# Reordering the opening of a fused attention-and-mixer kernel: the shift's row, the statistics and the first sums

## The chip, the cores and the metric

The kernel runs on one core of a Trainium2 chip. The core has a matrix engine (TensorE; its matmuls are "PE" in the profile and its weight loads "PEld"), a vector engine (VectorE, "DVE"), an engine for activations (ScalarE, "ACT"), GpSimd ("POOL") and SyncE ("SP"), which here issues most of the transfers. Each engine works through its own list of instructions in order, and engines wait for each other through semaphores. The metric is the device time of one execution in microseconds (us): before the change 448.7 us, the median of three runs from 448.26 to 449.26.

## The reference

The input x has 2048 tokens of 448 channels. Six vectors come from a condition c: `sa, ca, ga, sb, cb, gb`. Cut to what matters here:

```
mod = (silu(c) @ w_mod).reshape(1, 6, 1, 448)
h = layernorm(x) * (1 + ca) + sa
q, k, v = split(h @ wqkv)                     # 16 heads of 28
pq, pk = phi(q), phi(k)                       # phi(t) = t + 1 if t > 0 else exp(t), + 1e-6
o = (pq @ (pk^T v)) / (pq @ sum(pk) + 1e-6)
x = x + ga * (o @ wo)
h = layernorm(x) * (1 + cb) + sb
x = x + gb * mixer(h)                         # a token MLP, gelu between two products
```

The change lies in the first of these lines: the projection of k (the letter j = 1 in the code) and the sum over tokens of pk times the normalised x.

## The kernel before

The tokens are cut into 16 tiles of 128 (`NT`). A tile comes twice from memory: `X[t]` with tokens on the partitions and `XT[t]`, its transpose, in four pieces of channels, the last of 64 channels stored twice. Products are made to nearly full fp32 precision from fp32r halves: a "high" half, the rounded value, and a "low" half, the rest. `a_split(t)` makes `hh` (high, on ACT, L390) and `hl` (low, on DVE, L393) of `XT[t]`.

The layernorm is not applied to the input of the projection. The weights Wk are scaled by 1 + ca (`w_high`, `w_low`, L253 and L265), x itself is multiplied by them (`project(t, 1, "kp")`, ten matmuls, L410), and one more matmul of a few rows, `close(t, 1)` (L417), adds what mean and spread require. On its moving side stand the rows of `Wrow`: the column sums of the scaled weights and the product of the shift sa with Wk, "the shift's row". On its stationary side stand mean and deviation of each token, transposed. After that the tile only needs the factor 1/deviation per token, which `a_exp(t)` gives as a scale: an exp (L424) and a relu (L425) on ACT, read from the PSUM bank of the projection.

The shift's row is made in these steps: `col_acc(0)` (DVE) and `col_mm` (PE, L215 and L217) give sa as columns, `col_out(0)` copies them to SBUF (DVE, L225 to L227), the four `row_part(1, ch)` add Wk times these columns up (DVE, L271 once and L273 three times), `row_sum(1)` (PE, L280) and `row_bias(1)` (PE, L283) sum over the partitions into the bank `rowb`, and `row_out(1)` copies the rows to `Wrow` (ACT, L287) and cuts the second half (DVE, L288).

The statistics of a tile come in two forms. `a_stats_act` uses ACT: a pass that sums (L349), a pass that squares (L328), each with a readout of the accumulator; POOL scales the sums (L354, L355). `a_stats` uses DVE: `bn_stats` and `bn_aggr` (L364, L365) and an addition (L366). Both end in a power on POOL (L340) that gives deviation and its inverse, "the root", for one tile or two at once. Before the change ACT serves tiles 0, 1 and 4 (`ACT_STATS`), DVE all others. `a_rows(t)` writes mean and deviation with their rests into `rowst` (L373, L375): on POOL for the tiles in `ACT_STATS`, on DVE for the others. `a_transpose(t, n)` (PE, L383) turns the rows of one or two tiles in one bank, `a_copy(t)` (ACT, L386) puts them beside `hl` of the tile, where `close(t, 1)` finds them.

After `a_exp(t)`, `a_pk(t)` (DVE, L430) makes pk, `a_pk_parts(t)` its halves `pkh` (ACT, L478) and `pkl` (for tiles 0 and 1 on DVE, L480; for most others ACT and an accumulating transfer issued by POOL, L483), and a second transfer of POOL (L487) adds pk to a running sum. `a_norm(t)` (DVE, L458) normalises `X[t]` to `xn`, `a_high` (ACT, L462) and `a_low` (DVE, L467, L468) make its halves `xh` and `xl`. `a_outer(t)` (PE, L504) is "the sums" of a tile: eleven matmuls into four banks `cacc`, which stay in use until tile 15.

PSUM has eight banks, and each new bank waits until the last reader of its former tile is done; the SBUF tiles come from a pool of 74 slots in the same way. The order on each engine is the order of the program text. What is between the opening matmuls and the loop is written out by hand; then the loop over t from 4 to 15 projects tile t + 1, closes tile t, transposes t + 1, adds the sums of tile t - `KV_LAG` = t - 4, and lets ACT, DVE and POOL prepare the tiles ahead. The order on PE around the change, before it: project(0) to project(2), columns of sa, row_sum, project(3), transposes of 0 and 1, row_bias, transposes of 2 and 3, project(4), close 0 to 3, transpose of 4, and in the loop project(5), close(4), transpose of 5, sums of 0, project(6), close(5), transpose of 6, sums of 1, project(7).

Of the kernel before, what the change touches and what calls it, by code (L numbers as in the profile page):

```python
# [8 lines left out]
F32 = mybir.dt.float32  # L9
# [5 lines left out]
P = 128  # L15
# [12 lines left out]
Q_EARLY = {10: 0, 11: 1, 12: 2, 13: 3, 14: 4}  # L28
ACT_STATS = (0, 1, 4)
RING = 6  # L30
# [18 lines left out]
def block_kernel(ctx: ExitStack, tc: tile.TileContext, x, xt, wqkv, wo, w1, b1, w2, b2, c, wmod, wfirst, out):  # L49
# [29 lines left out]
    def split(full, hi, lo):  # L79
# [15 lines left out]
    nc.gpsimd.affine_select(out=m3, in_=m3, compare_op=ALU.is_ge, fill=0.0, base=DH - 1,  # L95
                            pattern=[[0, 4], [DH, 4], [0, DH]], channel_multiplier=-1)
    mhalf = cst.tile([P, 2], F32, name="mhalf")
    nc.vector.memset(mhalf, -0.5)
# [239 lines left out]
    def a_pow(g, ve):  # L338
        n = g.shape[1]
        nc.gpsimd.tensor_tensor(g[:, :, 1:3], ve, roots.unsqueeze(1).to_broadcast([P, n, 2]), op=ALU.pow)  # L340
# [18 lines left out]

    def a_stats(*ts):  # L360
        g, ve = a_group(ts)
        for t in ts:
            b6 = small.tile([P, 6], F32, name=f"st{t}", tag="st")
            nc.vector.bn_stats(b6, X[t])  # L364
            nc.vector.bn_aggr(mv[t][:, 0:2], b6)  # L365
        nc.vector.tensor_scalar_add(ve, g[:, :, 1:2].to_broadcast([P, len(ts), 2]), EPS)  # L366
        a_pow(g, ve)

    def a_rows(t):
        r = rowst[t % RING]  # L370
        pair = mv[t][:, 0:2]
        eng = nc.gpsimd if t in ACT_STATS else nc.vector
        eng.tensor_copy(r[:, 64:].rearrange("p (b c) -> p b c", b=2)[:, :, 0:2],  # L373
                              pair.unsqueeze(1).to_broadcast([P, 2, 2]))
        eng.tensor_sub(r[:, 66:68], pair, r[:, 64:66].bitcast(F32))  # L375

# [19 lines left out]
    def a_split(t):  # L396
        a_split_high(t)
        a_split_low(t)
# [13 lines left out]
    def project(t, j, name):  # L412
        projects([(t, kind, ch) for ch in range(3) for kind in ("hh", "wl", "hl")] + [(t, "hh", 3)], j, name)
# [111 lines left out]
    w_row(1)  # L525
    act2, act2_end = a_stats_act((0, 1))
    act2(0)
    col_acc(0)
# [3 lines left out]
    a_split(3)  # L532
    act2(1)
    act2_end()
    a_rows(0)
    a_rows(1)
    a_stats(2, 3)
    col_out(0, pc)
    for ch in range(4):
        row_part(1, ch)  # L540
    project(3, 1, "kp")
    a_transpose(0, 2)
    row_bias(1)
    a_split(4)
    a_rows(2)
    a_rows(3)
    act1, act1_end = a_stats_act((4,))
    act1(0)
    act1_end()
    a_rows(4)  # L550
    a_norm(0)
    a_stats(5)
    a_copy(0)
    a_copy(1)
    a_high(0)
    row_out(1)
    a_transpose(2, 2)
    load_xt(9)
# [3 lines left out]
    load_x(10)  # L562
    project(4, 1, "kp")
    a_copy(2)
    a_copy(3)
    a_split_high(5)
    a_low(0)
    a_split_low(5)
    kps = [close(t, 1) for t in range(4)]
    a_transpose(4)  # L570
    a_exp(0, kps[0])
    a_copy(4)
    a_rows(5)
    a_pk(0, kps[0])
    a_norm(1)
    a_pk_parts(0)
    a_exp(1, kps[1])
    a_pk(1, kps[1])
    a_stats(6)
    a_exp(2, kps[2])  # L580
    a_split_high(6)
    a_exp(3, kps[3])
    a_pk(2, kps[2])
    a_split_low(6)
    a_high(1)
    a_pk_parts(1)
    a_rows(6)
    a_low(1)
    a_pk(3, kps[3])
# [4 lines left out]
    for t in range(4, NT):  # L594
        if t + 1 < NT:
            project(t + 1, 1, "kp")
        kp = close(t, 1)
        if t + 1 < NT:
            a_transpose(t + 1)
        if t == 9:  # L600
            row_sum(0)
            row_bias(0)
        a_outer(t - KV_LAG)
        if t in Q_EARLY:
# [10 lines left out]
        a_phi_q(t in Q_EARLY)  # L615
        if t + 1 < NT:
            a_copy(t + 1)
# [635 lines left out]
```

## Time and profile before

| What | us |
|---|---|
| median of three runs | 448.7 |
| lowest and highest run | 448.26, 449.26 |
| the profiled execution's own time | 449.38 |
| its span in the trace | 447.7 |
| PE busy in it | 440.4 |
| DVE busy in it | 353.7 |
| ACT busy in it | 266.0 |
| POOL busy in it | 106.7 |

A row of a timeline gives the start and the duration in us, then the engine, the line of the kernel, the operation, the tile written and the tiles read, the shape, the count of merged instructions, and in brackets the idle time of the engine ahead of it with what ended that idle time. Durations of pipelined instructions overlap: from start to start is the time that an engine is occupied. The granted TensorE clock of the profiled execution is 1.0.

### The profile page before, as it was taken

The page shows a single profiled execution, that of the slowest core. Times are in us where ns is not written, and L with a number is a line of the kernel's source. Part 1 is how long each engine was busy: PE and PEld are TensorE (multiplying, and loading weights), DVE is VectorE, ACT ScalarE, POOL GpSimd, SP SyncE. Part 2 cuts the span into 40 slices and gives each one's busy share as a digit, 9 for nine tenths or more (in the row PEclk, how much of TensorE's full clock was granted, in tenths as well). Part 3 has the DMA queues.
Part 4 walks back from the last instruction along what each step waited for, and adds up shares of the span by engine and source line. Part 5 has one row for each costly group of instructions (what it writes and reads, how often), then busy time and mean ns, then how long its engine had stood idle before and what let it go on. Part 6 is the DMA issues. An engine that isn't in the chain of part 4 may idle for free.

```text
span 447.7 us, 7324 instructions
## 1 busy us (share of the span) xinstructions
PE 440.4 (98%) x2370; PEld 405.4 (91%) x2370; DVE 353.7 (79%) x798; ACT 266.0 (59%) x575; POOL 106.7 (24%) x195
## 2 busy tenths in 40 slices
PE   8989999999999999999999999999999999999997
PEld 7868889999899999989999999999999999999996
DVE  3978998679998899896467776649697788978873
ACT  4679978657757776767674444336554546356531
POOL 3346454300024355454300000000110211302101
PEclk9999999999999999999999999999999999999999
DMA  7997999545200003322416454227985668966333
GB/s 239 383 290 137 218 241 250 84 141 191 72 1 1 23 25 96 71 48 48 141 32 217 158 164 140 90 76 240 283 190 156 111 187 196 213 175 116 54 89 62
DMA packets 58854, 63.22 MB, mean 141 GB/s; under 512 B 5249, under 2 KB 49345, under 8 KB 58817
## 3 DMA queue, kind: packets, MB, share of 16 engines
q1 hardware_dynamic: 51616, 51.17, 37.6%
q0 software_dynamic: 7200, 11.60, 16.1%
q8 instruction: 18, 0.29, 0.3%
q14 instruction: 20, 0.16, 0.1%
HBM read 46.57 MB, written 7.34 MB: 120 GB/s over the span
## 4 chain that ended last, share of the span: by engine, by line
PE 92%; DMA 2%; ACT 2%; POOL 1%; SPq 1%; issue 1%; DVE 0%; ACTq 0%; POOLq 0%
PE y L1009 14%; PE up L817 10%; PE up L819 10%; PE up L818 10%; PE op L766 9%; PE cacc L504 7%; PE qp L410 7%; PE y L1010 7%; PE kp L410 5%; PE yp L817 3%; PE yp L818 2%; PE yp L819 2%; PE tq L750 2%; DMA wr<-in_qkv_dram 1%; DMA x<-in_A_x_dram 1%; PE qp L417 1%
## 5 line engine op out<-in xcount | busy, mean ns | idle before, releaser
L817 PE MATMUL up<-h2h,ph 128*128 128x448 f32 x224 | 81.3, 363 | 0.0
L819 PE MATMUL up<-h2h,pl 128*128 128x448 f32 x224 | 81.2, 363 | 0.0
L818 PE MATMUL up<-h2l,ph 128*128 128x448 f32 x224 | 80.8, 361 | 0.0
L81 DVE TENSOR_TENSOR pl<-pr,ph 128x512 fp32r<-128x512 f32 (+1 forms) x60 | 36.3, 616 | 14.2 <-ACT ph L80 10.3
L80 ACT ACTIVATE ph<-pr 128x512 fp32r<-128x512 f32 (+1 forms) x60 | 33.0, 570 | 24.0 <-PE up L818 17.7
L819 PEld LDWEIGHTS up<-h2h,pl 128*128 128x128 f32 x224 | 42.0, 188 | 3.1
L818 PEld LDWEIGHTS up<-h2l,ph 128*128 128x128 f32 x224 | 41.9, 187 | 3.0
L817 PEld LDWEIGHTS up<-h2h,ph 128*128 128x128 f32 x224 | 42.0, 188 | 2.4
L971 POOL DMA_DIRECT2D a<-a x12 | 10.6, 912 | 113.1 <-PE yp L819 97.0
L1029 POOL DMA_DIRECT2D out_dram<-yt x12 | 10.5, 872 | 83.1 <-DVE yt L1020 54.7
L1015 ACT ACTIVATE cc<-y 128x448 f32<-128x448 f32 x18 | 9.8, 546 | 25.5 <-PE y L1010 25.5
L766 PE MATMUL op<-wph,pth 112*128 112x448 f32 x64 | 24.5, 382 | 0.0
L504 PE MATMUL cacc<-pkh,xh 128*128 128x448 f32 x64 | 24.4, 381 | 0.0
L410 PE MATMUL kp<-wh,hh 128*128 128x448 f32 x64 | 23.0, 369 | 1.1 <-ACT rk L425 0.9
L410 PE MATMUL qp<-wh,hh 128*128 128x448 f32 x64 | 23.4, 365 | 0.0
L504 PE MATMUL cacc<-pkl,xh 128*128 128x448 f32 x64 | 23.3, 364 | 0.0
L766 PE MATMUL op<-wpl,pth 112*128 112x448 f32 x64 | 23.3, 363 | 0.0
L766 PE MATMUL op<-wph,ptl 112*128 112x448 f32 x64 | 23.2, 362 | 0.0
L754 ACT ACTIVATE pth<-tq 112x512 fp32r<-112x512 f32 x16 | 9.6, 599 | 17.6 <-PE tq L750 17.6
L817 PE MATMUL yp<-uw,qw 128*128 128x448 f32 x54 | 19.9, 369 | 0.0
L819 PE MATMUL yp<-uw,qw 128*128 128x448 f32 x54 | 19.6, 364 | 0.0
L818 PE MATMUL yp<-uw,qw 128*128 128x448 f32 x54 | 19.6, 363 | 0.0
(243 smaller groups left out, 1311.2 us busy)
## 6 DMA issues: line engine op xcount, KB each, us to landing
pr<-in_B_w_dram SPq DMA_DIRECT2D x48, 256.0 KB, 3.0
a<-in_B_w_dram SPq DMA_DIRECT2D x24, 256.0 KB, 5.3
a<-in_B_w_dram SPq DMA_DIRECT2D x24, 192.0 KB, 5.4
xt<-in_xt_dram SPq DMA_DIRECT2D x16, 256.0 KB, 4.9
x<-in_A_x_dram SPq DMA_DIRECT2D x16, 224.0 KB, 4.8
wm<-in_B_wmod_dram SPq DMA_DIRECT2D x16, 196.0 KB, 5.0
wr<-in_qkv_dram SPq DMA_DIRECT2D x12, 224.0 KB, 5.5
out_dram<-x SPq DMA_DIRECT2D x12, 224.0 KB, 2.0
```

The source lines that it names most:

```text
L80: nc.scalar.activation(hi, full, AF.Copy)
L81: nc.vector.tensor_sub(lo, full, hi.bitcast(F32))
L410: nc.tensor.matmul(pps[t, j][:, :D], a[:, ch * P:(ch + 1) * P], w, start=first, stop=False)
L504: nc.tensor.matmul(cacc[ch][:, :D], a[:, s], b, start=(t == 0 and i == 0), stop=(t == NT - 1 and i == len(todo) - 1))
L766: nc.tensor.matmul(opb[t][:, :D], a[:, s], b, start=(n == 0), stop=(n == 11))
L817: nc.tensor.matmul(ps[:, :D], hi[:, sl], mh, start=first, stop=False)
L818: nc.tensor.matmul(ps[:, :D], hi[:, sl], ml, start=False, stop=False)
L819: nc.tensor.matmul(ps[:, :D], lo[:, sl], mh, start=False, stop=last)
L971: nc.gpsimd.dma_start(w, a, accum_op=ALU.add)
L1009: nc.tensor.matmul(ps[:, :D], h[:, s], w, start=opens and r == 0, stop=False, skip_group_check=True)
L1010: nc.tensor.matmul(ps[:, :HD], l[:, s], wh, start=False, stop=closes and r == PAIRS - 1, skip_group_check=True)
L1029: nc.gpsimd.dma_start(of[t * P:(t + 1) * P, :], ysum.pop(t), accum_op=ALU.add)
```

## The change

The tiles' statistics change engines: ACT takes tiles 2 and 3, DVE takes tile 4 in one group with tile 5 (`a_stats_dve`, which splits the work into a part for each tile and an end with one root for both). All rows are now written by DVE. `col_out(0)` and the additions with Wk (`row_part`) keep their place after the statistics of tiles 0 and 1, but the statistics of tiles 2 and 3 on DVE are no longer ahead of them. Project(4), then the closing of tiles 0 and 1, come ahead of the transposes of 2 and 3; project(5) ahead of the closing of 2 and 3; the sums of tile 0 ahead of the transposes of tiles 4 and 5 (now a pair in one bank) and of project(6); close(4) after project(6). What the loop did in its turn t = 4 for PE, and project(6) of turn 5, is written out ahead of it. A tile of 160 bytes named `space` that nothing uses takes the room that the dropped small tiles leave, so that the addresses of the later tiles are those of before. The order on PE after it: project(3), transposes of 0 and 1, row_bias, project(4), close 0 and 1, transposes of 2 and 3, project(5), close 2 and 3, sums of 0, transposes of 4 and 5, project(6), close(4), close(5), transpose of 6, sums of 1, project(7).

```diff
--- before.py
+++ after.py
@@ -26,7 +26,6 @@
 KV_LAG = 4
 HIGH_AT = {13: (11, 12), 14: (13,), 15: (14, 15)}
 Q_EARLY = {10: 0, 11: 1, 12: 2, 13: 3, 14: 4}
-ACT_STATS = (0, 1, 4)
 RING = 6
 FETCH = {4: 11, 5: 12, 7: 13, 9: 14, 10: 15}
 SUM_DMA = range(2, 13)
@@ -94,6 +93,7 @@
                             pattern=[[0, 4], [-DH, 4], [0, DH]], channel_multiplier=1)
     nc.gpsimd.affine_select(out=m3, in_=m3, compare_op=ALU.is_ge, fill=0.0, base=DH - 1,
                             pattern=[[0, 4], [DH, 4], [0, DH]], channel_multiplier=-1)
+    cst.tile([P, 40], F32, name="space")
     mhalf = cst.tile([P, 2], F32, name="mhalf")
     nc.vector.memset(mhalf, -0.5)
     roots = cst.tile([P, 2], F32, name="roots")
@@ -357,22 +357,30 @@
             a_pow(g, ve)
         return one, end
 
-    def a_stats(*ts):
+    def a_stats_dve(ts):
         g, ve = a_group(ts)
-        for t in ts:
-            b6 = small.tile([P, 6], F32, name=f"st{t}", tag="st")
-            nc.vector.bn_stats(b6, X[t])
-            nc.vector.bn_aggr(mv[t][:, 0:2], b6)
-        nc.vector.tensor_scalar_add(ve, g[:, :, 1:2].to_broadcast([P, len(ts), 2]), EPS)
-        a_pow(g, ve)
+
+        def one(i):
+            b6 = small.tile([P, 6], F32, name=f"st{ts[i]}", tag="st")
+            nc.vector.bn_stats(b6, X[ts[i]])
+            nc.vector.bn_aggr(mv[ts[i]][:, 0:2], b6)
+
+        def end():
+            nc.vector.tensor_scalar_add(ve, g[:, :, 1:2].to_broadcast([P, len(ts), 2]), EPS)
+            a_pow(g, ve)
+        return one, end
+
+    def a_stats(t):
+        one, end = a_stats_dve((t,))
+        one(0)
+        end()
 
     def a_rows(t):
         r = rowst[t % RING]
         pair = mv[t][:, 0:2]
-        eng = nc.gpsimd if t in ACT_STATS else nc.vector
-        eng.tensor_copy(r[:, 64:].rearrange("p (b c) -> p b c", b=2)[:, :, 0:2],
+        nc.vector.tensor_copy(r[:, 64:].rearrange("p (b c) -> p b c", b=2)[:, :, 0:2],
                               pair.unsqueeze(1).to_broadcast([P, 2, 2]))
-        eng.tensor_sub(r[:, 66:68], pair, r[:, 64:66].bitcast(F32))
+        nc.vector.tensor_sub(r[:, 66:68], pair, r[:, 64:66].bitcast(F32))
 
     tps = {}
 
@@ -523,84 +531,93 @@
               (1, "wl", 0), (1, "wl", 1), (1, "wl", 2), (1, "hl", 0), (1, "hl", 1), (1, "hl", 2)], 1, "kp")
     project(2, 1, "kp")
     w_row(1)
-    act2, act2_end = a_stats_act((0, 1))
-    act2(0)
+    act01, end01 = a_stats_act((0, 1))
+    act01(0)
     col_acc(0)
     pc = bank("col0")
     col_mm(pc, macc.pop(0), one, True, True)
     row_sum(1)
     a_split(3)
-    act2(1)
-    act2_end()
-    a_rows(0)
-    a_rows(1)
-    a_stats(2, 3)
+    act01(1)
+    end01()
     col_out(0, pc)
     for ch in range(4):
         row_part(1, ch)
+    a_rows(0)
+    a_rows(1)
     project(3, 1, "kp")
     a_transpose(0, 2)
     row_bias(1)
     a_split(4)
+    a_norm(0)
+    dve45, end45 = a_stats_dve((4, 5))
+    dve45(0)
+    act23, end23 = a_stats_act((2, 3))
+    act23(0)
+    act23(1)
+    end23()
+    a_copy(0)
+    a_copy(1)
+    row_out(1)
     a_rows(2)
     a_rows(3)
-    act1, act1_end = a_stats_act((4,))
-    act1(0)
-    act1_end()
-    a_rows(4)
-    a_norm(0)
-    a_stats(5)
-    a_copy(0)
-    a_copy(1)
     a_high(0)
-    row_out(1)
-    a_transpose(2, 2)
     load_xt(9)
     load_x(9)
     load_mod(2)
     load_xt(10)
     load_x(10)
     project(4, 1, "kp")
+    a_split(5)
+    a_low(0)
+    kps = [close(t, 1) for t in (0, 1)]
+    a_transpose(2, 2)
+    project(5, 1, "kp")
+    a_exp(0, kps[0])
+    a_pk(0, kps[0])
+    dve45(1)
+    end45()
     a_copy(2)
     a_copy(3)
-    a_split_high(5)
-    a_low(0)
-    a_split_low(5)
-    kps = [close(t, 1) for t in range(4)]
-    a_transpose(4)
-    a_exp(0, kps[0])
-    a_copy(4)
-    a_rows(5)
-    a_pk(0, kps[0])
+    kps += [close(t, 1) for t in (2, 3)]
+    a_exp(1, kps[1])
     a_norm(1)
     a_pk_parts(0)
-    a_exp(1, kps[1])
+    a_outer(0)
     a_pk(1, kps[1])
-    a_stats(6)
+    a_rows(4)
+    a_rows(5)
+    a_transpose(4, 2)
     a_exp(2, kps[2])
     a_split_high(6)
-    a_exp(3, kps[3])
     a_pk(2, kps[2])
     a_split_low(6)
+    a_exp(3, kps[3])
     a_high(1)
+    a_copy(4)
+    a_copy(5)
+    project(6, 1, "kp")
+    kps.append(close(4, 1))
+    a_stats(6)
     a_pk_parts(1)
+    a_low(1)
     a_rows(6)
-    a_low(1)
     a_pk(3, kps[3])
     a_pk_parts(2)
     a_stats(7)
     wo_sb = []
     late = [t for t in range(NT) if t not in Q_EARLY.values()]
     for t in range(4, NT):
-        if t + 1 < NT:
+        if 5 < t < NT - 1:
             project(t + 1, 1, "kp")
-        kp = close(t, 1)
-        if t + 1 < NT:
+        kp = close(t, 1) if t > 4 else kps[4]
+        if 4 < t < NT - 1:
             a_transpose(t + 1)
         if t == 9:
             row_sum(0)
             row_bias(0)
-        a_outer(t - KV_LAG)
+        if t > 4:
+            a_outer(t - KV_LAG)
         if t in Q_EARLY:
             a_q(Q_EARLY[t])
         if t == 12:
@@ -613,7 +630,7 @@
         if 7 < t + 3 < NT:
             a_stats(t + 3)
         a_phi_q(t in Q_EARLY)
-        if t + 1 < NT:
+        if 4 < t < NT - 1:
             a_copy(t + 1)
         a_exp(t, kp)
         if t + 3 < NT:
```

## The prediction

> **What bounds the kernel now.** I read the page first, then the waits of PE (TensorE's matmuls), then the timelines of the engines between 16 and 45 us. All times are us from the start of the span; "tile t" is token tile t.
>
> ```profile
> span 447.7 us, 7324 instructions
> ...
> PE 440.4 (98%) x2370; PEld 405.4 (91%) x2370; DVE 353.7 (79%) x798; ACT 266.0 (59%) x575; POOL 106.7 (24%) x195
> ```
>
> PE is busy for 98% of the span, so an edit that leaves PE's work as it is can win only where PE stands still. The waits of PE over the whole span say where:
>
> ```profile
> PE kp L410 <- ACT rk L425: 0.9, 1, 0.9
> PE rw L383 <- DVE rowst L373: 0.9, 1, 0.9
> ```
>
> Beside the first matmul of the span and two waits of 0.3 us or less before 11 us, the list has only these two and one for POOL's rows, which the timeline below splits into 0.27 and 0.40. All of it, 2.4 us, lies in the stage that the diff rewrites (the bracket is the idle time before the row and what ended it):
>
> ```profile
> 21.05 0.37 PE L410 MATMUL kp<-wh,hh 128*128 128x448 f32 x1
> 21.68 0.32 PE L383 MATMUL rw<-ident,rowst 128*98 128x128 f32 x1 [0.27 <-POOL rowst L375]
> 22.40 0.32 PE L383 MATMUL rw<-ident,rowst 128*98 128x128 f32 x1 [0.40 <-POOL rowst L375]
> 22.55 0.92 PE L283 MATMUL rowb<-accb,sel_b 128*98 128x448 f32 x2
> 24.32 0.50 PE L383 MATMUL rw<-ident,rowst 128*98 128x128 f32 x2 [0.86 <-DVE rowst L373]
> ...
> 26.77 1.08 PE L417 MATMUL kp<-wrow,hl 98*128 98x448 f32 x4
> ...
> 30.49 0.47 PE L504 MATMUL cacc<-pkl,xh 128*128 128x448 f32 x1
> ...
> 33.63 0.48 PE L410 MATMUL kp<-wh,hh 128*128 128x448 f32 x1 [0.87 <-ACT rk L425]
> ...
> 39.15 0.47 PE L410 MATMUL kp<-wh,hl 128*128 128x448 f32 x1
> ```
>
> Project(3) ends at 21.25 (its last matmul starts at 21.05 and the next could start 0.2 later). The transposes of tiles 0 and 1 wait for POOL's rows, those of tiles 2 and 3 for DVE's; project(6) waits until exp(3) has read its bank. The row at 39.15 is the third matmul of project(7); I measure the lead there. The chain of waits gives the price of PE's work when nothing is missing:
>
> ```profile
> 45.89 2.21 PE cacc L504 x11
> 48.09 2.03 PE kp L410 x10
> ```
>
> So a matmul of 448 columns is 0.20, a projection 2.03, the eleven sums of a tile 2.21. The two pairs follow each other without a gap, and the list of PE's waits has nothing later than 33.63: what PE gains before project(7) should reach the end of the span.
>
> **Part 1: the shift's row earlier.** The diff takes the statistics of tiles 2 and 3 off DVE (they go to ACT), so that col_out(0) and the four additions follow straight after a_split(3). Rows 0 and 1 go from POOL to DVE.
>
> ```profile
> 17.54 0.27 PE L217 MATMUL col<-ones,acc 128*64 128x128 f32 x1
> ```
> ```profile
> 17.58 0.62 DVE L364 BATCH_NORM_STATS2 st<-x 128x6 f32<-128x448 f32 x1
> ...
> 19.48 0.16 DVE L226 COPY col<-col 128x3 f32<-128x3 f32 x1
> ...
> 20.17 2.12 DVE L273 SCALAR_TENSOR_TENSOR accb<-wr,col,accb 128x448 f32<-128x448 f32 x3
> ...
> 23.81 0.17 DVE L373 CAST rowst<-mv 128x4 fp32r<-128x4 f32 x1 [0.92 <-POOL mv L340]
> 24.02 0.16 DVE L375 TENSOR_TENSOR rowst<-mv,rowst 128x2 fp32r<-128x2 f32 x1
> 24.09 0.16 DVE L373 CAST rowst<-mv 128x4 fp32r<-128x4 f32 x1
> ```
> ```profile
> 18.89 1.29 POOL L340 TENSOR_TENSOR mv<-ve,roots 128x4 f32<-128x4 f32 x1
> ```
>
> DVE is free at 17.58; the column that it copies is complete on PE at 17.81. I start the copy at 17.95 in place of 19.48; from there to the end of the additions is 22.29 - 19.48 = 2.81, so they end at 20.76. The roots of tiles 0 and 1 are there at 20.18. A tile's row costs DVE 0.28 (23.81 to 24.09) and PE's transpose starts 0.30 after the second instruction of a row (24.02 to 24.32). Row 0 starts at 20.68, row 1 at 20.96, its second instruction at 21.17: transposes at 21.27 and 21.5 instead of 21.68 and 22.40, the biased row at 21.65 instead of 22.55. PE is free again at the latest 0.92 after that; I take 22.5 for project(4), which needs nothing of tiles 2 and 3 and ends at 24.53.
>
> **Part 2: closing 0 and 1 first.** Close(0) needs the row copied out by ACT, then cut by DVE, behind the statistics that ACT got:
>
> ```profile
> 18.34 0.19 ACT L328 ACTIVATION_READ_ACCUMULATOR junk<-x,as 128x1 f32 x1
> ...
> 18.95 0.56 ACT L349 ACTIVATE junk<-x 128x448 f32<-128x448 f32 x1
> ...
> 20.45 0.19 ACT L328 ACTIVATION_READ_ACCUMULATOR junk<-x,as 128x1 f32 x1
> 22.75 0.44 ACT L386 ACTIVATE hl<-rw 34x128 fp32r<-34x128 f32 x2 [2.11 <-PE rw L383]
> ...
> 25.51 0.54 ACT L287 ACTIVATE wrow<-rowb 34x448 fp32r<-34x448 f32 x1
> ```
> ```profile
> 26.09 0.63 DVE L288 TENSOR_TENSOR wrow<-rowb,wrow 2x448 fp32r<-2x448 f32 x1 [0.25 <-ACT wrow L287]
> ```
>
> One tile's statistics occupy ACT for about 1.6 (18.95 to 20.54). Two end at 22.13, where ACT stands idle now (the bracket of 2.11), so the added tile costs nothing; without that idle time it would cost 1.6. Two copies end at 22.58, the row leaves ACT at about 23.35 and DVE at 24.0: 0.5 before project(4) ends. POOL needs 1.65 from the end of ACT's last read (18.53 to 20.18 for tiles 0 and 1), so the roots of 2 and 3 are there at 23.9, and DVE's rows 2 and 3 at 24.5. PE then runs without a wait: close 0 and 1 from 24.53, two transposes, project(5) from 25.25 to 27.28, close 2 and 3 to 27.68.
>
> **Part 3: the first sums ahead of tile 4.** They need tile 0 to go through the whole chain:
>
> ```profile
> 27.34 0.64 ACT L424 ACTIVATE ek<-kp,mv 128x448 f32<-128x448 f32 x1 [0.30 <-PE kp L417]
> 27.87 0.63 ACT L425 ACTIVATE rk<-kp,mv 128x448 f32<-128x448 f32 x1
> ```
> ```profile
> 28.54 0.63 DVE L430 SCALAR_TENSOR_TENSOR pk<-ek,rk 128x448 f32<-128x448 f32 x1 [0.22 <-ACT rk L425]
> ...
> 29.81 0.63 DVE L480 SCALAR_TENSOR_TENSOR pkl<-pk,pkh 128x448 fp32r<-128x448 f32 x1 [0.22 <-ACT pkh L478]
> ```
>
> Close(0) to exp(0) is 0.57 (26.77 to 27.34), and exp and relu take 0.53 each of ACT's time (27.34 to 27.87). So exp(0) at 25.10, ACT free at 26.16; then the copies of 2 and 3 (0.45), exp(1) (1.06), and pkh(0) from 27.67 to 28.25, and pkl(0) follows it on DVE by 0.03: 28.28 to 28.91. The second sum starts 0.05 after that (30.44 to 30.49): 28.95. Behind close(3) PE therefore idles from 27.68 to 28.95, less 0.2 for the first sum: this order makes a **new wait of about 1.1**, and the transposes of 4 and 5 and project(6) are queued behind it. The remaining ten sums and a hiccup end at 31.05, two transposes at 31.35. A root of 4 and 5 begun at about 27.9 is done at 29.2, the rows at 29.9, so they are in time. Project(6) needs the bank that exp(2) or exp(3) reads; behind pkh(0) ACT has both, with one other copy between, done by 30.8. It starts at 31.35 against 33.63: 2.28 less, of which close(4) is still owed (0.2).
>
> From here DVE, not PE, sets the pace, because its low half of tile 7 arrives just when PE wants it:
>
> ```profile
> 36.51 0.62 DVE L364 BATCH_NORM_STATS2 st<-x 128x6 f32<-128x448 f32 x1
> ...
> 37.45 0.51 DVE L458 TENSOR_SCALAR xn<-x,mv 128x448 f32<-128x448 f32 x1
> 37.88 0.62 DVE L430 SCALAR_TENSOR_TENSOR pk<-ek,rk 128x448 f32<-128x448 f32 x1
> 38.42 0.68 DVE L393 TENSOR_TENSOR hl<-xt,hh 128x512 fp32r<-128x512 f32 x1
> ```
>
> Statistics take 0.94 of DVE, xn 0.43, pk 0.54, hl 0.6. After pkl(0) DVE has pk(1), rows 4 and 5, pk(2), hl6 and statistics 6 (to 32.1), pkl(1) behind ACT's copies of 4 and 5 (32.6 to 33.1), low(1) 0.6, row 6 0.28, pk(3), statistics 7, xn(2), pk(4): hl7 from 36.5 to 37.15, against 38.42 to 39.10. PE has project(6) to 33.38, two closes to 33.8, transpose 6 at 34.1, the sums to 36.45, and its third matmul of project(7) at 36.85 must wait for 37.15. **Lead at that row: 39.15 - 37.15 = 2.0.** DVE's moved work cancels: two tiles' statistics leave it (1.7), one comes (0.8) with three rows (0.84).
>
> The unused 160-byte tile is never written and costs nothing; the loads keep their order on SP's queue. Bounds of what the trace doesn't show: the new wait could shrink to 0.6 (pkh(0) alone) or grow by the 0.6 that a root can lengthen (rows below). Lead 1.4 to 2.5.
>
> On POOL next to DVE the trace has two roots of one tile:
>
> ```profile
> 25.91 0.72 POOL L340 TENSOR_TENSOR mv<-ve,roots 128x2 f32<-128x2 f32 x1 [0.26 <-DVE ve L366]
> ...
> 37.71 1.33 POOL L340 TENSOR_TENSOR mv<-ve,roots 128x2 f32<-128x2 f32 x1
> ```
>
> The second overlaps pk(4) and hl7 above: it is 0.6 longer, while DVE's two keep 0.62 and 0.68. The Trainium skill ("SBUF — State Buffer", Who interferes with whom) says that a VectorE instruction with two SBUF inputs and a GpSimd one that reads SBUF exclude each other, the later one blocked until the first ends. By that rule pkl(0) would wait out the root of 4 and 5, and the lead would be 1.0; the trace agrees for POOL's side only, so my sum leaves DVE free.
>
> **The rivals.**
> - **POOL's root holds DVE.** A root begun at 27.9 keeps pkl(0), two SBUF inputs, until 29.2: the second sum at 29.9 instead of 28.95, 0.95 lost, lead 1.05, time 447.65. For it: the 0.6 above shows that they interfere. Against it: in the rows DVE lost nothing.
> - **The lead is given back.** In the loop's later turns accumulating DMAs hold DVE:
>
> ```profile
> 73.27 0.63 DVE L430 SCALAR_TENSOR_TENSOR pk<-ek,rk 128x448 f32<-128x448 f32 x1 [1.45 <-DMA pk<-pk]
> ```
>
>   If those landings stay where they are while all else comes 2.0 earlier, waits grow by 2.0 and the time is 448.7. Against it: this 1.45 costs PE nothing today, and those DMAs are issued behind work that moves too.
> - **Slower: tile slots run short in turns 5 to 8.** The new order keeps other tiles alive, and a wait like that of 1.45 on DVE would there have no cover, since hl7 comes 0.05 before PE takes it. Two of them cost 2.9 against 2.0 won: 449.6. It decides once such waits before 58 us exceed 2.0. Against it: today the first one on DVE comes after 60 us, and the tiles of a turn are the same.
>
> **How the numbers follow.** The profiled execution took 449.38, its span 447.7 with 1.7 around it; the sum makes it 447.4. That run is 0.7 above the median of 448.7, so the forecast is 448.7 - 2.0 = 446.7. A change of 0.2% (0.9 us) is about what a measurement here can tell from none. Chances: forecast 0.62 (own range 446.2 to 447.3, from the leads), POOL's root 0.15, given back 0.11, slower 0.12. Faster 0.77, same 0.11, slower 0.12. The range, 445.9 to 448.2, takes in the first rival and the better half of the second.
>
> **What would show it.** Right: transposes 0 and 1 before 21.7, project(4) before 22.7 with no idle time until close(3), one wait of about 1.1 at the first sums, released by ACT's pkh and DVE's pkl, project(6) near 31.4, the third matmul of project(7) near 37.2, PE's later timeline the same and 2.0 earlier. Wrong: pkl(0) starting only at the end of POOL's root; DVE waits for DMAs before 58; a wait of close(0) for the row's cut on DVE; a first sum later than 30.

## The result and the profile after

| | median, us | range, us | runs | ratio to the kernel before, 95% interval |
|---|---|---|---|---|
| before | 448.44 | 447.96 to 449.59 | 20 | |
| after | 447.38 | 446.86 to 448.55 | 20 | 0.9976 [0.9969, 0.9983] |

The changed kernel is faster by 1.06 us, 0.24%. The forecast was 446.7 and a lead of 2.0: the direction is right and the time lies in the range, but half of the lead is missing. The profiled execution of the kernel after took 448.35, its span 446.2.

The page and the list of PE's waits (us in total, times, the longest), kernel after:

```profile
span 446.2 us, 7331 instructions
...
PE 439.1 (98%) x2370; PEld 405.5 (91%) x2370; DVE 353.5 (79%) x801; ACT 267.5 (60%) x580; POOL 104.3 (23%) x188
```
```profile
PE kp L418 <- ACT wh L253: 1.1, 1, 1.1
...
PE cacc L512 <- ACT pkh L486: 0.3, 1, 0.3
PE rw L391 <- DVE rowst L383: 0.3, 1, 0.3
...
PE cacc L512 <- DVE pkl L488: 0.2, 1, 0.2
```

The waits of 0.9, 0.9 and 0.7 for exp(3)'s bank, DVE's rows and POOL's rows are gone. In their place stand the new wait at the first sums, in two parts, and a short one for a row. Of the lines left out (`...`) two matter little to the stage: 0.6 ahead of the columns of the opening (0.2 before), and a new 0.2 at a transpose behind 117 us. One number grew with which the diff has nothing to do: the first projection waits 1.1 for the split weights, where the profile of before had 0.3. The timeline of PE, kernel after (start, duration, and in the bracket the idle time before the row and what ended it):

```profile
11.43 0.47 PE L418 MATMUL kp<-wh,hh 128*128 128x448 f32 x1 [1.10 <-ACT wh L253]
...
22.18 0.43 PE L391 MATMUL rw<-ident,rowst 128*98 128x128 f32 x2
22.45 0.92 PE L283 MATMUL rowb<-accb,sel_b 128*98 128x448 f32 x2
22.85 0.71 PE L418 MATMUL kp<-wh,hh 128*128 128x448 f32 x1
23.40 0.37 PE L418 MATMUL kp<-wl,hh 128*128 128x448 f32 x1
...
28.09 0.57 PE L425 MATMUL kp<-wrow,hl 98*128 98x448 f32 x2
29.00 0.47 PE L512 MATMUL cacc<-pkh,xh 128*128 128x448 f32 x1 [0.34 <-ACT pkh L486]
29.66 0.47 PE L512 MATMUL cacc<-pkl,xh 128*128 128x448 f32 x1 [0.19 <-DVE pkl L488]
...
31.91 0.45 PE L418 MATMUL kp<-wh,hh 128*128 128x448 f32 x1
...
34.92 0.29 PE L391 MATMUL rw<-ident,rowst 128*98 128x128 f32 x1 [0.33 <-DVE rowst L383]
...
37.87 0.47 PE L418 MATMUL kp<-wh,hl 128*128 128x448 f32 x1
```

From the transposes of 0 and 1 to the closing of 3 there is no bracket, as forecast (the third matmul of project(5) starts 0.31 behind the second in place of 0.20, so 0.1 is lost there). Behind that closing (28.09, two matmuls, so the next could start at 28.49) the first sum starts at 29.00 and the second, possible at 29.20, at 29.66: 0.51 and 0.46, together 0.97 of idle time against the forecast's 1.07. The third matmul of project(7) is at 37.87 where it was 39.15: 1.28 earlier. What follows it keeps that: from it to the end of the span are 408.55 before (447.7 - 39.15) and 408.33 after (446.2 - 37.87).

Everything in this timeline before 28 us is later than forecast, because this execution opened later. The two kernels' rows of the opening, ACT's and PE's timelines, before:

```profile
7.76 0.63 ACT L390 ACTIVATE hh<-xt 128x512 fp32r<-128x512 f32 x1 [3.61 <-DMA xt<-in_xt_dram]
...
14.72 0.58 ACT L349 ACTIVATE junk<-x 128x448 f32<-128x448 f32 x1 [1.55 <-DMA x<-in_A_x_dram]
```
```profile
10.50 0.47 PE L410 MATMUL kp<-wh,hh 128*128 128x448 f32 x1 [0.28 <-ACT wh L253]
```

and ACT's timeline after:

```profile
8.69 0.63 ACT L398 ACTIVATE hh<-xt 128x512 fp32r<-128x512 f32 x1 [4.55 <-DMA xt<-in_xt_dram]
...
15.17 0.58 ACT L349 ACTIVATE junk<-x 128x448 f32<-128x448 f32 x1 [1.07 <-DMA x<-in_A_x_dram]
```

Two loads set these two openings. The first split waits for XT0's landing (7.76 and 8.69) and the first projection follows it by 2.74 (10.50 and 11.43); the statistics of tile 0 wait for X0's (14.72 and 15.17). Neither load was moved by the diff. The stage from the first projection to the third matmul of project(7) took 28.65 before (39.15 - 10.50) and 26.44 after (37.87 - 11.43). That is 2.21 shorter, a little more than the forecast's 2.0, while the matmul itself came only 1.28 earlier and the medians differ by 1.06. The experiments ask which opening each kernel hangs on, and then which part of the diff carries the gain.

### The profile page after: what moved, and what is told of

It is laid out like the page before. It is cut to its first block, busy times and chain, and to the rows that moved or that the text cites. A ratio compares the mean times of both kernels' runs of the same rounds, so it can differ in the third digit from the quotient of the medians.

```text
span 446.2 us, 7331 instructions
## 1 busy us (share of the span) xinstructions
PE 439.1 (98%) x2370; PEld 405.5 (91%) x2370; DVE 353.5 (79%) x801; ACT 267.5 (60%) x580; POOL 104.3 (23%) x188
## 4 chain that ended last, share of the span: by engine, by line
PE 91%; ACT 3%; DVE 2%; POOL 1%; DMA 1%; issue 1%; SPq 0%; ACTq 0%
PE y L1026 14%; PE up L836 10%; PE up L835 10%; PE up L834 9%; PE cacc L512 7%; PE qp L418 7%; PE op L783 7%; PE y L1027 7%; PE kp L418 6%; PE yp L834 2%; PE yp L836 2%; PE yp L835 2%; PE tq L767 1%; DMA xt<-in_xt_dram 1%; PE qp L425 1%
## 5 line engine op out<-in xcount | busy, mean ns | idle before, releaser
L1046 POOL DMA_DIRECT2D out_dram<-yt x12 | 10.5, 874 | 82.3 <-DVE yt L1037 53.9
```

Source lines behind the costliest of these rows:

```text
L1046: nc.gpsimd.dma_start(of[t * P:(t + 1) * P, :], ysum.pop(t), accum_op=ALU.add)
```

## The experiments

Each ratio is to the kernel before as it ran beside that kernel, on the same chip.

### Both kernels once more

Both files unchanged, to have a second opening of each.

> The kernel before, unchanged, for a second look at its opening. In its first profile PE's first projection started at 10.50 and the third matmul of project(7) at 39.15, 28.65 later; in the profile after the change these are 11.43 and 37.87, 26.44 later. So the edited stage is 2.2 shorter there, while the medians differ by 1.06 only. Theory M (the stage gives 2.0 to 2.2 whatever the opening does; XT0 landed 0.93 later in the one profile by chance, or because of something in the changed program): the distance is 28.65 plus or minus 0.2 again; if the landing is chance, the start of the first projection scatters between 10.4 and 11.5 here too. Theory L (the lead depends on the opening: what the transfers set stays where it is): the distance shrinks by what the opening is late. Time ratio 1.000.

> The changed kernel, unchanged, for a second look at its opening. Theory M: the distance from the first projection to the third matmul of project(7) is 26.4 plus or minus 0.2 whatever the opening; if the late XT0 was chance, the first projection may start near 10.5 and the whole is then 2 us below a run of before with the same opening. Theory L: with a first projection near 10.5 the distance is about 27.5, since x0's landing and ACT's statistics do not move with PE. If the landing is late again (11.3 or more) and before_again's is early, the changed program itself delays the opening. Time ratio 0.9965 to 0.9985, the measured one.

Measured: before 448.55 (ratio 1.0002 [0.9993, 1.001]), after 447.33 (0.9971 [0.9962, 0.998]; 448.56 - 447.33 = 1.23). The timelines of before's second profile, PE and ACT:

```profile
11.00 0.47 PE L410 MATMUL kp<-wh,hh 128*128 128x448 f32 x1 [0.63 <-ACT wh L253]
...
21.76 0.28 PE L383 MATMUL rw<-ident,rowst 128*98 128x128 f32 x1
22.44 0.32 PE L383 MATMUL rw<-ident,rowst 128*98 128x128 f32 x1 [0.40 <-POOL rowst L375]
...
39.19 0.47 PE L410 MATMUL kp<-wh,hl 128*128 128x448 f32 x1
```
```profile
14.76 0.58 ACT L349 ACTIVATE junk<-x 128x448 f32<-128x448 f32 x1 [1.09 <-DMA x<-in_A_x_dram]
```

and those of after's second:

```profile
10.59 0.47 PE L418 MATMUL kp<-wh,hh 128*128 128x448 f32 x1 [0.21 <-ACT wh L253]
...
21.34 0.41 PE L391 MATMUL rw<-ident,rowst 128*98 128x128 f32 x2
...
37.02 0.47 PE L418 MATMUL kp<-wh,hl 128*128 128x448 f32 x1
```
```profile
14.36 0.58 ACT L349 ACTIVATE junk<-x 128x448 f32<-128x448 f32 x1 [1.10 <-DMA x<-in_A_x_dram]
```

The kernel before opened 0.50 later than in its first profile (11.00 against 10.50), and nothing came of it: the wait of the first transpose (0.27 in the prediction's rows) is gone, the second transpose stands at 22.44 where it stood at 22.40, and project(7)'s third matmul at 39.19 where it stood at 39.15. Its waits for rows soak up a late opening. What both profiles share is the distance from X0's statistics: 39.15 - 14.72 and 39.19 - 14.76 are both 24.43. X0 landed at nearly the same time in both, so the agreement alone proves little; the rows of before's first profile give the chain. ACT works without a wait from 14.72 to its last read of tile 1's statistics, which ends at 18.53; POOL's root of 0 and 1 starts at 18.89, its rows of 0 and 1 take it to 22.30 and its root of 2 and 3 to 23.78, DVE cuts the rows at 23.81, and the transposes of 2 and 3 follow at 24.32. The kernel after has no such cushion; from its first projection the same matmul is 26.44 (37.87 - 11.43) and 26.43 (37.02 - 10.59) away. So **before is timed by X0's landing, after by the start of its first projection**, which in these profiles follows XT0's landing, and the lead is

(X0's statistics + 24.43) - (first projection + 26.44) = (X0's statistics - first projection) - 2.01.

By the opening of before's first profile that gives 14.72 - 10.50 - 2.01 = 2.21, by its second 14.76 - 11.00 - 2.01 = 1.75. Of the readings quoted above each holds for one kernel: theory L for before, whose distance shrank from 28.65 to 28.19 as it opened 0.50 later, and theory M for after. The gain does depend on the opening, but it is the kernel before that stays put when XT0 is late, and the one after that moves.

### Moving one load or the other

If that is so, an earlier X0 should help before and not after, and a later XT0 should hurt after and not before. The same two edits were made in both kernels. X0 earlier:

```diff
     load_xt(2)
-    load_first(0)
     load_x(0)
-    load_xt(3)
+    load_first(0)
     load_x(1)
+    load_xt(3)
```

> The kernel before with the load of X0 issued ahead of the four pieces for sa, and X1 ahead of XT3. Two profiles of before start their first projection at 10.50 and 11.00 but reach the third matmul of project(7) at 39.15 and 39.19, with X0 landed (ACT's first statistics) at 14.72 and 14.76. Theory A (before is timed by X0's landing, through ACT's statistics, POOL's roots and the rows; the changed kernel by XT0's landing, through PE): ACT's statistics start at 13.2 to 13.8, the transposes of 0 to 3 come 0.5 to 0.8 earlier, and the time is 0.5 to 1.0 below before. Theory B (both are timed by XT0 and the equal arrival of project(7) was chance): nothing changes, within 0.3.

> The changed kernel with the same two loads moved. Theory A: PE has no wait between its first projection and the first sums in that kernel, so X0's landing is not what it waits for: within 0.3 of the changed kernel, and the distance between the two kernels shrinks to 0.3 to 0.9. Theory B: both move alike.

XT0 later:

```diff
     load_first(1)
+    load_qkv(1, chs=(3, 0))
     load_xt(0)
-    load_qkv(1, chs=(3, 0, 1, 2))
+    load_qkv(1, chs=(1, 2))
```

> The kernel before with XT0 issued behind two pieces of Wk instead of ahead of all four, so that the first projection starts about 1.0 later (11.5 to 12.0). Theory A: the waits for rows take most of it up, 0 to 0.5 slower than before. Theory B: the whole 1.0 appears in the time.

> The changed kernel with XT0 issued behind two pieces of Wk. Theory A and theory B: the first projection starts about 1.0 later and so does all of PE's work up to project(7), 0.8 to 1.2 slower than the changed kernel; under A the two kernels with a late XT0 are then within 0.6 of each other, under B they stay 1.1 apart.

| kernel | median, us | ratio, interval | first projection | X0's statistics | project(7), third matmul |
|---|---|---|---|---|---|
| before, beside them | 448.59 | | | | |
| before, X0 early | 448.19 | 0.9989 [0.9981, 0.9998] | 10.31 | 12.89 | 38.56 |
| after, X0 early | 447.33 | 0.9972 [0.9962, 0.9983] | 11.15 | 13.73 | 37.59 |
| before, XT0 late | 449.07 | 1.0011 [1.0003, 1.002] | 11.78 | 14.36 | 39.00 |
| after, XT0 late | 448.43 | 0.9997 [0.9989, 1.0006] | 11.77 | 14.35 | 39.78 |

X0 early took 0.40 off before and nothing off after (447.33 with it, 447.33 and 447.38 without). XT0 late cost before 0.48 and after 1.10 (448.43 - 447.33). With X0 early the kernel after keeps its 26.44 (37.59 - 11.15). Compared under the same edit, the change gains 0.86 with X0 early (448.19 - 447.33) and 0.64 with XT0 late (449.07 - 448.43), both less than 1.06 and 1.23; for XT0 late the formula gives 0.57 (14.36 - 11.78 - 2.01). The directions are those of the formula. Three sizes need a word.

Before should have stayed put with XT0 late, and it lost 0.48. In its profile no wait for rows is left: beside the first projection's 1.25, PE waits 0.3 for the additions with Wk and 0.8 for exp(3)'s bank. An opening as late as 11.78 has used up the cushion.

Before gained less from X0 than the 0.5 to 1.0 expected. The ACT timeline of that kernel (before, X0 early) shows what came next:

```profile
12.89 0.56 ACT L349 ACTIVATE junk<-x 128x448 f32<-128x448 f32 x1
...
15.68 0.63 ACT L390 ACTIVATE hh<-xt 128x512 fp32r<-128x512 f32 x1 [1.11 <-DMA xt<-in_xt_dram]
```

The edit brought X0's statistics 1.83 forward (14.72 to 12.89), but XT3, put behind X1, now ends ACT's wait at 15.68 (so 24.43 does not hold there), and the third matmul came only 0.59 earlier (39.15 to 38.56).

After with XT0 late lost more in its profile than the opening: project(7)'s third matmul is 28.01 behind the first projection (39.78 - 11.77), not 26.44. Its PE timeline and one window of 2 us (PE, PEld, DVE, ACT and POOL busy, PE's granted clock, DMA share, GB/s):

```profile
11.77 0.64 PE L419 MATMUL kp<-wh,hh 128*128 128x448 f32 x1 [1.69 <-ACT wh L254]
```
```profile
12.00:14.00 2.00, 2.00 (x6) 1.78 (x6) 2.00 (x4) 2.00 (x5) 0.00 (x0) 0.50 1.06 393
```

PE is busy all the time and starts 6 matmuls in 2 us; the granted clock is 0.50. In before with XT0 late, PE idled 1.25 ahead of its first projection and the clock stayed at 1.00. The profiled execution of after with XT0 late is the exception among its twelve: its mean clock is 0.996 and its span 448.0, while the other eleven have 0.999 to 1.000 and 445.7 to 447.0. So the 1.10 of the medians comes from the later opening, and the clock has little part in it. The next two experiments ran into the same effect in most executions.

### Parts of the change alone

**The first sums late**: the kernel after with the sums of tile 0 put back behind project(6).

```diff
     a_pk_parts(0)
-    a_outer(0)
     a_pk(1, kps[1])
...
     project(6, 1, "kp")
+    a_outer(0)
     kps.append(close(4, 1))
```

> The changed kernel with the sums of tile 0 back behind project(6). The transposes of tiles 4 and 5 then wait for their rows (DVE's last row instruction at 30.54 in the profile after the change) behind close(3), which ends at 28.5. If the sums ahead of tile 4 are worth what the prediction's steps say, PE idles about 2.2 there in place of 0.97, and part of that is given back because hl7 on DVE limits project(7): 1.0 to 1.3 slower than the changed kernel, so 0 to 0.4 slower or faster than before. If the order of the sums does not matter because DVE sets the pace of project(7) anyway (rival), the time is that of the changed kernel within 0.3.

**The row alone**: part 1 of the change (additions ahead of the statistics, DVE's rows) with before's order of closings, transposes and sums. The diff is against the kernel after:

```diff
     a_rows(3)
+    dve45(1)
+    end45()
     a_high(0)
+    a_transpose(2, 2)
...
     project(4, 1, "kp")
-    a_split(5)
+    a_copy(2)
+    a_copy(3)
+    a_split_high(5)
     a_low(0)
-    kps = [close(t, 1) for t in (0, 1)]
-    a_transpose(2, 2)
-    project(5, 1, "kp")
+    a_split_low(5)
+    a_rows(4)
+    kps = [close(t, 1) for t in range(4)]
+    a_transpose(4)
...
```

> The kernel before with the first part of the change alone: additions with Wk ahead of the statistics, tiles 2 and 3 on ACT, tiles 4 and 5 on DVE, all rows on DVE, but the old order of the closings and sums. The prediction's steps say that the transposes of 0 and 1 no longer wait (0.67 won) but those of 2 and 3 wait longer, until rows that DVE writes at 24.6 to 25.1, so that the start of project(4) moves from 24.6 to about 25.0 for the same opening: 0 to 0.6 slower than before. The rival, that the earlier row alone brings the gain and the order of the closings adds little: 0.7 to 1.1 faster than before.

Measured: sums late 450.58 (ratio 1.0044 [1.0028, 1.006]), row alone 450.67 (1.0039 [1.0026, 1.0053]). Both are some 2 us slower than before, far outside what was expected. PE's timeline and one window of 2 us, sums late:

```profile
29.49 0.56 PE L391 MATMUL rw<-ident,rowst 128*98 128x128 f32 x2 [1.92 <-DVE rowst L381]
...
32.14 0.57 PE L418 MATMUL kp<-wl,hh 128*128 128x448 f32 x1
32.51 0.57 PE L418 MATMUL kp<-wh,hl 128*128 128x448 f32 x1
...
35.11 0.36 PE L512 MATMUL cacc<-pkh,xl 128*128 128x448 f32 x1
35.31 0.36 PE L512 MATMUL cacc<-pkh,xh 128*128 128x448 f32 x1
```
```profile
32.00:34.00 2.00, 2.00 (x6) 1.74 (x6) 1.92 (x7) 1.05 (x3) 1.06 (x2) 0.50 0.11 42
```

and row alone:

```profile
24.27 0.56 PE L391 MATMUL rw<-ident,rowst 128*98 128x128 f32 x2 [1.80 <-DVE rowst L381]
...
25.14 0.57 PE L418 MATMUL kp<-wl,hh 128*128 128x448 f32 x1
25.51 0.57 PE L418 MATMUL kp<-wh,hl 128*128 128x448 f32 x1
```
```profile
26.00:28.00 2.00, 2.00 (x7) 1.78 (x6) 1.25 (x5) 0.00 (x0) 0.81 (x1) 0.50 1.05 253
```

The waits are as one would reckon them: rows 4 and 5 are cut on DVE at 28.98, as in the kernel after (30.06, with a first projection 1.07 later), whether sums stand in front of them or not, and rows 2 and 3 at 24, because PE was done earlier and the rows were not. What wasn't reckoned with is the sequel: matmuls start 0.37 apart where 0.20 is usual, for some 3.4 us. Not every execution shows it: the mean clock is 0.996 in five of the six of sums late and 0.995 or 0.996 in four of the six of row alone. The other three keep 1.000 and took 449.07 (sums late), 448.98 and 449.75 (row alone).

**The same two with the idle time filled.** To part the order's own cost from the clock's, matmuls that nobody reads were put into the idle time, nine of 128 columns in the one and eight in the other (the profile records each as two). The edit of the first:

```diff
+    fill = bank("fill")
+    for i in range(9):
+        nc.tensor.matmul(fill[:, :P], ones, ones, start=True, stop=True)
     a_transpose(4, 2)
```

> The kernel with the sums of tile 0 behind project(6), plus nine 128-column matmuls of no use where PE stood idle for 1.92 ahead of the transposes of 4 and 5 (they add work that nothing reads). In its profile the granted clock was 0.50 from 32 to 34 and 448-column matmuls started 0.37 apart from about 31 to 35, after that idle time. If the idle time made PE slow for about 3.5 us, filling it takes away 1.5 to 1.8 and leaves 448.8 to 449.2, that is 1.3 to 1.7 above the changed kernel, what the order alone costs. If the slow stretch has another cause, the time stays at 450.6.

> The kernel with the first part of the change alone, plus eight 128-column matmuls of no use in the idle 1.80 ahead of the transposes of 2 and 3. Its profile had a granted clock of 0.68 and 0.50 between 24 and 28. If the idle time brought that on, the time falls from 450.7 to 448.9 to 449.2, 0.3 to 0.6 above before, as the prediction's steps have it for this part alone. If not, it stays at 450.7.

Measured: sums late, filled 448.98 (1.0011 [1.0002, 1.0019]); row alone, filled 449.35 (1.0015 [1.0006, 1.0024]); before beside them 448.41. PE's timeline, sums late filled, then row alone filled:

```profile
28.25 2.17 PE L591 MATMUL fill<-ones 128*128 128x128 f32 x18
30.33 0.57 PE L391 MATMUL rw<-ident,rowst 128*98 128x128 f32 x2
...
43.79 0.47 PE L418 MATMUL kp<-wh,hl 128*128 128x448 f32 x1 [0.40 <-DVE hl L401]
```
```profile
22.22 1.95 PE L569 MATMUL fill<-ones 128*128 128x128 f32 x16
24.19 0.56 PE L391 MATMUL rw<-ident,rowst 128*98 128x128 f32 x2
```

The filling delays nothing (30.33 against 29.49 with a first projection at 11.20 against 10.36, so 0.84 later in both; 24.19 against 24.27 with 10.47 against 10.54), the mean granted clock is 1.000 again where it was 0.996 and 0.995, and 1.6 and 1.3 us come off the medians (by the ratios, since the chips differ, 1.5 and 1.1). The executions that kept their clock without any filling, 449.07, 448.98 and 449.75, lie near the filled medians. So the clock cost about that much, and what is left is the order's:

- The late sums cost 1.6 beside the kernel after (448.98 against 447.33 and 447.38), as expected. Two places in the profile hold it: the third matmul of project(7), at 38.69, is 27.49 behind the first projection against 26.44, and a wait of 0.40 for DVE's low half of tile 8 comes at 43.79, which the kernel after doesn't have.
- The row alone brings no gain: it is 0.7 slower than before by the ratio (0.3 to 1.1 by its interval), where 0.3 to 0.6 was expected. Its rows 2 and 3 are cut at 23.68, where before had them at 23.81: ACT now takes the statistics of four tiles one after the other, and POOL's root comes behind them. PE stands there instead of at the earlier rows, and the wait of 0.86 for exp(3)'s bank is as it was (33.42, for 33.63).

So the earlier row alone brings nothing, and with it the order of the first sums decides between a loss and the gain. Whether the new order would gain without the earlier row was not tried.

### Two attempts on the new wait and on the opening

**pk's halves first**: the kernel after with pkh(0) and pkl(0) ahead of exp(1), to shorten the new wait.

```diff
     kps += [close(t, 1) for t in (2, 3)]
+    a_pk_parts(0)
     a_exp(1, kps[1])
     a_norm(1)
-    a_pk_parts(0)
     a_outer(0)
```

> The changed kernel with the halves of pk(0) made ahead of exp(1) on ACT and ahead of xn(1) on DVE, to shorten the new wait of the first sums. pkh(0) then starts when pk(0) is done (27.5 in the profile after, not 28.38), pkl(0) behind the statistics of tile 5 at 28.4, the second sum at 29.1 instead of 29.66. Behind it project(6) waits for the bank of exp(3), which ends no earlier than now, so of the 0.6 about 0.3 is left: 0.2 to 0.4 faster than the changed kernel. If DVE alone sets the pace of project(7), 0 to 0.1.

Measured: 447.87 (0.9985 [0.9976, 0.9994]), not faster than after. PE's timeline:

```profile
28.46 0.47 PE L512 MATMUL cacc<-pkl,xh 128*128 128x448 f32 x1 [0.17 <-DVE pkl L488]
...
31.39 0.47 PE L418 MATMUL kp<-wh,hh 128*128 128x448 f32 x1 [0.43 <-ACT rk L433]
...
34.55 0.29 PE L391 MATMUL rw<-ident,rowst 128*98 128x128 f32 x1 [0.46 <-DVE rowst L383]
...
37.50 0.47 PE L418 MATMUL kp<-wh,hl 128*128 128x448 f32 x1
```

PE's wait for ACT's pkh at the first sum is gone, and ACT's exps, pushed back by the half, hold project(6) by 0.43 at the same bank as in the kernel before. Row 6 is later too. From the first projection (10.88) it is 26.62 to project(7), against 26.44: the stage is balanced between its waits.

**The column first**: the kernel after with tile 0's low half on DVE behind the column of scales, which the weights' split needs, so that a late XT0 holds less.

```diff
-    a_split(0)
+    a_split_high(0)
     col_mm(pc, macc.pop(1), one, False, True)
     keep_warm(5)
     col_out(1, pc)
+    a_split_low(0)
```

> The changed kernel with the low half of tile 0 (DVE) put behind col_out(1), so that XT0's landing no longer holds the columns of 1 + ca and with them the scaled weights. From the profile after the change: XT0 lands at 8.69, hl0 runs to 10.0, col_out at 9.96, the first projection at 11.43, while col_mm is done at 9.0. If the changed kernel is timed by XT0's landing (theory A), the first projection starts at 10.3 to 10.5 in nearly every execution, 0.1 to 1.0 earlier depending on the landing, the median 0.2 to 0.5 below the changed kernel's 447.35, and the distance from the first projection to the third matmul of project(7) stays 26.4. If the projection's start then waits for the weights Wk from memory instead, nothing changes.

Measured: 447.08 (0.9968 [0.9958, 0.9977]), the best median of all, but its interval overlaps those of after. In its profile XT0 landed early (split at 7.40), so it doesn't show the case for which the edit was made. The first projection came at 10.94 all the same, not at 10.3 to 10.5 as expected, and the matmul of project(7) 26.40 behind it. DVE's timeline shows what held the column of scales now, although the low half no longer stands ahead of it:

```profile
9.46 0.16 DVE L223 TENSOR_SCALAR col<-col 128x4 f32<-128x4 f32 x1 [1.67 <-PE col L217]
```

It waited for PE's sums of that column (`col_mm`). So the first projection has a second thing to wait for beside XT0. Whether the edit is worth anything stays open; it is a few tenths at most.

## Why the prediction was half right

**Part 1, the row.** Right. In after's second profile, with an opening 0.09 later than the one that the prediction used, the transposes run back to back from 21.34 (forecast 21.27 and 21.5), the biased row is at 21.60 (21.65), and project(4) starts at 22.00 and ends at 24.36 (22.5 and 24.53).

**Part 2, closing first.** Right: no idle time from project(4) to the closing of 3, but for the 0.1 in project(5).

**Part 3, the new wait.** Right in place and releasers, and 0.97 for 1.07. Project(6), 0.93 taken off for the opening, is at 30.98, against 31.35: the sums of tile 0 ended 0.20 sooner (30.85 for 31.05), and the two transposes took 0.13 of PE's time ahead of it, not 0.3. Transpose 6 waits 0.33 for its row. The third matmul of project(7), which starts 0.43 behind the second instead of 0.20, lies at 36.94 by the same opening, against 37.15. DVE does set the pace there, as forecast.

**The step that failed** is the sum's last: "Lead at that row: 39.15 - 37.15 = 2.0", and "448.7 - 2.0". The start of before was read from one execution, in which XT0 had landed early and X0 4.22 behind the first projection, the start of after was reckoned from the same opening, and their difference was taken off the median as if every execution opened so. The prediction saw that this execution was 0.7 above the median, and did not ask in which stage the 0.7 lay. The prediction had the rows for the doubt: the waits for POOL's and DVE's rows are a cushion, and a kernel that loses its cushions pays for each late landing from then on. The mechanism of the stage was right and the term mis-sized: 2.21 by that opening if the kernel after kept its 26.44 there, 1.75 by the second, 1.06 and 1.23 in the medians. Over the ten profiles with X0 and XT0 issued in the usual order, X0's statistics lie 2.96 to 4.22 behind the first projection, and the opening that the prediction used is the largest of them. The measured gains fit a distance of 3.1 to 3.2 (2.01 more than 1.06 and 1.23); pk's halves first has 3.23, the column first 3.17, sums late filled 2.96, and the others lie at 3.67 and above.

The spans of all executions, most of them without a profile, point the same way. The 107 executions of before that ran beside the experiments or as its repetition have a median span of 446.7, and only four reach 447.6; the two executions whose profiles are read here have 447.7 and 447.6. The 30 executions of after have a median of 445.5, and its two profiles lie on both sides of it (446.2 and 445.2). So both profiles of before show executions about 1.0 longer than usual. An estimate from the spans: with 408.5 and 408.3 from project(7)'s third matmul to the end, as in the profiles, a usual execution of before has that matmul at 38.2 and one of after at 37.2, which are 1.0 apart. The row at 39.15, from which the forecast reckoned its lead, lies 0.9 to 1.0 later than the usual one.

That the measured 447.38 lies 0.68 from the forecast while the lead is 0.94 short is chance in part: the median of before came out at 448.44 in 20 runs, not at 448.7. The prediction's own range for its mechanism, 446.2 to 447.3, was just missed; the wider range, which took in the first rival as well, held it.

**What stays open.** Most profiles lie at 3.7 to 3.8, for which the formula gives 1.7 to 1.8; that is 0.5 to 0.7 more than the medians show. The three with 2.96 to 3.23 open in another way: DVE's column of scales waits 0.47 (pk's halves first), 1.67 (the column first) and 0.94 (sums late filled) for PE's sums, and the first projection comes 3.30 to 3.77 behind XT0's split, where it is 2.74 to 2.83 in the other seven. The medians fit such openings, but how the executions without a profile opened is not on record. Nor do openings explain all of before: 38.2 would need X0's statistics at 13.8 (38.2 - 24.43), and no profile with the usual order of loads has them below 14.11. Nor was an opening of 4.22 seen in the kernel after, where X0 rather than XT0 might time it.

**The rivals.** *POOL's root holds DVE*: no. The timelines of POOL and DVE, after:

```profile
28.54 1.20 POOL L340 TENSOR_TENSOR mv<-ve,roots 128x4 f32<-128x4 f32 x1 [4.16 <-DVE ve L369]
```
```profile
28.37 0.51 DVE L466 TENSOR_SCALAR xn<-x,mv 128x448 f32<-128x448 f32 x1
28.98 0.63 DVE L488 SCALAR_TENSOR_TENSOR pkl<-pk,pkh 128x448 fp32r<-128x448 f32 x1
29.53 0.62 DVE L438 SCALAR_TENSOR_TENSOR pk<-ek,rk 128x448 f32<-128x448 f32 x1
```

Pkl(0), with two inputs in SBUF, starts at 28.98 inside the root, which runs to 29.74 (spans on POOL are rough in a profile), and takes its usual 0.63, so that it ends at 29.61, ahead of the root. The Trainium skill ("SBUF — State Buffer", Who interferes with whom) would have the later of the two blocked until the first ends; by that rule this row would start at 29.74 at the earliest, and the measurement decides against it here.

*The lead is given back*: no, the distances to the end of the span, 408.55 and 408.33, show it kept. *Slower by tile slots*: no, DVE's first wait for a DMA behind the opening comes at 59.91, and is 0.49 long. None of the rivals named what did happen, that the kernel before has slack against the opening which the one after lacks.

## What to carry to other kernels

Before a lead is read off one execution, ask on which arrival each kernel's path begins: a wait that the change removes may have been the cushion for a late landing elsewhere, and the gain is then the smaller, the later that landing comes. Compare the openings of several executions where the edited stage lies close behind the first loads. Compare, too, the span of the execution that was profiled with the spans of the others: a lead reckoned from one that is longer than usual need not be there in the others. When an edit makes PE stand idle for as long as the 1.7 to 1.9 us of these runs, look at the granted clock behind it, or give PE something to do.

## What the runs showed of the hardware

The granted clock of PE fell to 0.50 after one idle stretch of 1.69, 1.80 or 1.92 us (after with XT0 late, row alone, sums late), and the slow stretch was 3.3 to 3.4 us long each time: from 11.8 to 15.2, 24.7 to 28.1 and 31.8 to 35.1. In the last it began 2.3 after the idle time had ended. Not every execution of these three kernels had it: one of twelve, four of six and five of six, by their mean clocks. Idle stretches of 1.25 (before with XT0 late) and 1.10 (after) brought none in their profiles. In that time 448-column matmuls started 0.37 apart in place of 0.20; filling the idle time restored the clock and 1.6 and 1.3 us, as said above. The Trainium skill ("TensorE: Matmul & The Clock Gate", Part 1: The HAM clock gate) puts the half rate behind an idle window of about 3.4 us. The length of the slow stretch agrees with its figure for a busy window; the idle time that brought it on was here only about half as long as the page has it. Where the limit lies wasn't tried, nor what beside the length of the idle time decides it, since the same kernel kept its clock in some executions and lost it in others (how long PE stood idle in those without a profile is not on record).
